# Last four output tiles in emptied weight buffers, the last tile copied by two engines, and a re-planned instruction order

## Chip, cores and metric

The kernel runs on one core of one Trainium2 chip. The metric is the device time of one execution in microseconds; for the kernel before it is 155.75 us (median of 13 runs, 154.97 to 156.91).

The core's engines are PE (TensorE, matrix multiplication, with PEld for its weight loads), DVE (VectorE), ACT (ScalarE), POOL (GpSimd) and SP (SyncE, which issues nearly all transfers here). Each engine works through its own instructions in the order in which they were written for it. Transfers between the chip's main memory (DRAM) and on-chip memory (SBUF) run on 16 DMA queues. PE writes its results to PSUM, which has eight banks.

## What is computed

A gated linear recurrence over 768 steps (4 batches, 8 heads, head size 48), followed by a gated MLP with a mix over the sequence. Cut to what matters:

```python
# q, k, v, alpha: (4, 8, 768, 48)
for t in range(S):
    state = alpha[:, :, t, :, None] * state + np.einsum('bhd,bhe->bhde', k[:, :, t], v[:, :, t])
    y[:, :, t] = np.einsum('bhd,bhde->bhe', q[:, :, t], state)
x = y.transpose(0, 2, 1, 3).reshape(4, 768, 384)

h = np.maximum(x @ w_in, 0.0)                  # w_in: (384, 1024)
u, v = h[..., :512], h[..., 512:]
v_n = (v - mean(v)) / sqrt(var(v) + 1e-6)      # over the last axis
v_s = np.einsum('ts,bsd->btd', w_spatial, v_n) + b_spatial[None, :, None]   # w_spatial: (768, 768)
out = (u * v_s) @ w_out                        # w_out: (512, 384); out: (4, 768, 384), float32
```

## The kernel before

**First stage.** Each batch's sequence is cut into 6 chunks of 128 steps, 24 chunks in all. For each chunk alpha, k, q and v are loaded (`ac`, `kc`, `qc`, `vc`). The decay is handled by logarithms: ACT takes `ln` (`la`), PE sums it along the chunk (`cum`), ACT takes the two exponentials (`binv`, and `cum` in place), POOL multiplies k by one (`kt`), DVE multiplies q by the other (`qt`). PE transposes both (`pt`), the result is copied to SBUF (`kqT`, operation `ev`), PE multiplies them (`sc`), DVE applies the causal mask (`ptm`), and PE forms the chunk's output `y` from the masked scores, v and the state carried over. The carried state is made in three operations of `state_update`: `z` on DVE (line 331, the sum of the old state and the chunk's update), `S` (line 338, the scaling by the chunk's decay, on POOL) and `sb` (line 344, two half copies into `sbd`, on POOL or DVE). Chunks 0 to 5 (batch 0) go in pairs through `pair`, the others singly through `first`. `finish_x` copies `y` out (`xs`), transposes it and stores it as the batch's `xT` (`xe`).

**Second stage.** For each batch PE multiplies `xT` by the two halves of `w_in` (groups `v` and `u`). `v` is normalised (`bn`, `rs`, `vn`), mixed over the sequence by `w_spT` (group `s`), given its bias on DVE (`vsb`) and multiplied by `u` on POOL (`g`, giving `gT`). Group `o` multiplies `gT` by `w_out`; there are 24 output tiles of 128 rows, 6 a batch. All these groups go through the helper `group`, so their matrix multiplications all stand on line 775. Each output tile is copied from PSUM to SBUF by ACT (line 960, recorded as line 207 of the helper `copy`), and SP issues its store (line 967).

**Buffers of output tiles.** `out_tile` (line 935) says where tile n goes. Tiles 0 to 7 go into `raw_w`, a ring of two buffers that held the weights as they were loaded, four tiles to a buffer. Tiles 8 to 10 go into `w_row`, which held `w_spatial`. Tiles 11 to 23 go into `o_sb`, a ring of four buffers, so that a tile from 15 on waits for the store of the tile four before it. The list `free` in `second_o` (line 951) tells the planner of this.

**The order.** Nothing above is issued in the order in which it is written. Every piece of work is an `Op` with the engines that may do it and a planned duration for each (`ENGINES`, line 76, holds some), its dependencies and a priority. `schedule` (line 96) then plans greedily: at each step, of all operations that could start, it takes the one with the smallest planned start (plus half the duration where several engines may do it, plus the operation's own `wait`, which `PATIENCE`, line 75, sets by kind), and emits it on that engine. So a changed number can change the order on every engine. Where PE has a planned gap before `WARM` (40 us), the planner fills it with multiplications of a constant tile `junk` (line 199), whose results are not used.

**Loads in the plan.** `dma` (line 305) makes two operations, the issue on SP and the transfer, with a planned time and a planned latency (`lat`, 1.9 by default). `PIECES` (line 89) says after which load of a chunk each weight is fetched; `w_out` comes after chunk 7's `qc`. The issue of the fetch gets that load's issue as a dependency (`late`, line 1000).

Of the kernel before, what the change touches and what calls it, by code (L numbers as in the profile page):

```python
# [51 lines left out]
class Clock:  # L52
# [19 lines left out]
        return end  # L72


PATIENCE = {"ev": -0.3, "v": -0.1, "g": -0.3, "sb": 0.3, "bb": 0.5, "ln": 0.2, "z": -0.2, "we": -0.1, "S": 0.2, "cast": -0.1, "rs": 0.1, "trk": -0.1, "xs": -0.3}
ENGINES = {
    "kt": {"POOL": 0.87},
    "vb": {"POOL": 0.47, "ACT": 0.42},
    "S": {"POOL": 0.57},
    "sb": {"POOL": 0.79, "DVE": 0.36},  # L80
    "vn": {"DVE": 0.33},
    "xe": {"ACT": 0.38},
# [1 line left out]
    "u": {"ACT": 0.38, "DVE": 0.47},  # L84
    "o": {"ACT": 0.38},
}
PAIRS = (0, 1, 2)
ACT_STATS = ((2, 2), (1, 4), (3, 4))
PIECES = {
    "w_in": ((0, "vc", 0, 0.35), (0, "kc", 2, 0.15)),  # L90
    "w_sp": ((0, "vc", 4, 0.35), (0, "qc", 6, 0.25), (0, "qc", 6, 0.25)),
    "w_out": (0, "qc", 7, 0.25),
}


# [45 lines left out]
def kernel(  # L141
# [14 lines left out]
    B, H, S, D = q.shape  # L156
# [3 lines left out]
    DM = H * D  # L160
    DFF = moe_w_in.shape[1]
    DH = DFF // 2
    NT = S // 128
# [12 lines left out]
    LD, LP, WT, ST = 0.97, 1.46, 2.35, 0.8  # L176
# [28 lines left out]
    def copy(eng, out, in_):  # L205
        if eng == "ACT":
            nc.scalar.copy(out=out, in_=in_)  # L207
        else:
            ENG[eng].tensor_copy(out=out, in_=in_)  # L209
# [81 lines left out]
    def op(key, *args, **kw):  # L291

        users = kw.pop("use", ())
        o = Op(*args, **kw)
        for s in users:
            s.users.append(o)
        ops.append(o)
        made[key] = o
        o.wait = PATIENCE.get(key[0], 0.0)
        return o  # L300

    def got(*keys):
        return [made.get(x) for x in keys]

    def dma(key, us, emit, deps, prio, eng="SP", issue=0.99, lat=1.9):
        o = op(key + ("issue",), eng, issue, emit, deps, prio=prio)
        return op(key, "DMA", us, lambda _: None, [o], prio=prio, lat=lat)
# [9 lines left out]
    def state_update(i, ndeps):  # L317

        c = i % NCH
        st = T[i]  # L320
        P = float(10 * i)
        sbd = sbd_bufs[i % NB]

        def z(_):
            st["state"] = work.tile([128, HP, D], FP32, name="state")
            if c == 0:
                nc.vector.tensor_copy(out=st["state"], in_=st["tp"])
            else:
                nc.vector.tensor_tensor(out=st["state"], in0=st["tp"], in1=T[i - 1]["state"], op=ALU.add)  # L329

        op(("z", i), "DVE", 0.27, z, got(("upd", i), ("S", i - 1), ("sb", i - WK)), prio=P + 8, use=[st["sl_t"]])

        def sf(eng):
            ENG[eng].tensor_tensor(  # L334
                out=st["state"], in0=st["state"], in1=st["bc"][:, :, None].to_broadcast([128, HP, D]),
                op=ALU.mult)

        op(("S", i), ENGINES["S"], None, sf, got(("z", i), ("ebc", i)), prio=P + 8)

        def sb(eng):  # L340
            copy(eng, sbd[0:64, :, 0:D], st["state"][0:64])
            copy(eng, sbd[64:128, :, D:2 * D], st["state"][64:128])

        op(("sb", i), ENGINES["sb"], None, sb, got(("S", i), ("y", i - NB + 1), ("cz", 1)), prio=P + 8.1)

    def finish_x(i):
# [20 lines left out]
        def xe(eng):  # L367
            if c == 0:
                tiles(b)
            to, fr = bt[b]["xT"][:, :, t0:t0 + C], st["xv"]  # L370
            if i // 2 in PAIRS:
                to = to.rearrange("p k (t two) -> p k t two", two=2)
# [6 lines left out]
    def io_users(x, j, back=None):  # L379

        j = j - IO if back is None else j
        if x == "cum":
            return got(("cum", 2 * j), ("cum", 2 * j + 1), ("cump", j, 0), ("cump", j, 1))
        return got((x, 2 * j), (x, 2 * j + 1), (x + "p", j), (x + "p", j, 0), (x + "p", j, 1))
# [205 lines left out]
    def first(i):  # L590
# [3 lines left out]
        st = T[i]  # L594
        P = float(10 * i)

        def load(name, src):
            def emit(_):
                if i % 2 == 0:
                    T[i + 1][name + "2"] = st[name + "2"] = io_pool.tile([128, 2, H, D], FP32, name=name)  # L600
                t = st[name] = st[name + "2"][:, i % 2]
                nc.sync.dma_start(out=t, in_=src[b, :, t0:t0 + C, :].rearrange("h s d -> s h d"))
            return emit

        j = i // 2
        jo = j - NKP
        dma(("ac", i), LD, load("ac", alpha), io_users("ln", j), P)
        dma(("kc", i), LD, load("kc", k), io_users("kt", j), P + 0.1)
        dma(("qc", i), LD, load("qc", q), io_users("qt", j), P + 0.2)
        dma(("vc", i), LD, load("vc", v), io_users("vb", j), P + 0.3)  # L610

        la, kt, qt = [x[j % NKP][:, i % 2].rearrange("p (hp s) d -> p hp s d", s=2) for x in (lap_bufs, ktp_bufs, qtp_bufs)]

# [51 lines left out]
        hold = {}  # L665
# [88 lines left out]
    def group(key, mms, per, deps, prio, evac, eng, dur, edeps=(), parts=2, pdeps=None):  # L754

        hold = {}
        sl = Slot(rings["p2"])
        n = -(-len(mms) // parts)
        prev = None
        for j in range(parts):  # L760
            part = mms[j * n:(j + 1) * n]

            def emit(_, part=part, j=j):
                if j == 0:
                    hold["ps"] = bank(pp_2, [128, 512], FP32, name="ps2")
                for m in part:
                    m(hold["ps"])

            prev = op(key + ("mm", j), "PE", per * len(part), emit,
                      list(deps) + [prev] + (pdeps[j] if pdeps else []),  # L770
                      prio=prio, take=sl if j == 0 else None, use=[sl], cols=per * len(part) * 2350)
        return op(key, eng, dur, lambda e: evac(e, hold["ps"]), [prev] + list(edeps), prio=5.0, use=[sl])

    def mm(out, lhsT, rhs, start, stop):
        return lambda ps: nc.tensor.matmul(out=out(ps), lhsT=lhsT(), rhs=rhs(), start=start, stop=stop)  # L775
# [34 lines left out]
    def second_v(b, tt):  # L810
# [3 lines left out]
        t0 = tt - tt % 2  # L814
        on_act = (b, t0) in ACT_STATS

# [117 lines left out]

    def out_tile(n):

        if n < 8:
            if n % 4 == 0:
                kept["t"] = raws.tile([128, 4 * DM], FP32, name="raw_w")
            return kept["t"][:, n % 4 * DM:(n % 4 + 1) * DM]  # L940
        if n < KEEP:
            return raws.tile([128, S], BF16, name="w_row", bufs=NROW).bitcast(FP32)
        return outp.tile([128, DM], FP32, name="o_sb")

    def second_o(b, tt):
        mms = [mm(
            lambda ps: ps[:, 0:DM], lambda dsl=dsl: bt[b]["gT"][:, dsl, tt * 128:(tt + 1) * 128],
            lambda dsl=dsl: w_out_sb[:, dsl, :], dsl == 0, dsl == NDS - 1) for dsl in range(NDS)]
        hold = {}
        n = b * NT + tt  # L950
        if n < 8:
            free = [made[("cast", "w_out", x)] for x in range(NDS)] + [made[("cast", "w_sp", 2, x)] for x in range(2)]
        elif n < KEEP:
            free = got(("wt", n - 8 + 3))
        else:
            free = got(("st", (n - 4) // NT, (n - 4) % NT)) if n >= KEEP + 4 else []

        def evac(eng, ps):
            hold["o"] = out_tile(n)
            copy(eng, hold["o"], ps[:, 0:DM])  # L960

        Q = 1000.0 + 100 * b + 30 + tt
        group(("o", b, tt), mms, 0.165, [made[("g", b, x, tt // 3)] for x in range(NDS)] + made[("w_out",)], Q, evac,
              ENGINES["o"], None, free, parts=1)

        def store(_):
            nc.sync.dma_start(out=out[b, tt * 128:(tt + 1) * 128, :], in_=hold["o"])

        dma(("st", b, tt), ST, store, got(("o", b, tt)), -1.0, issue=0.8)
        if n < KEEP:  # L970
            late.extend((made[("st", b, tt, "issue")], (x, N - 1, "issue")) for x in ("ac", "kc", "qc", "vc"))
        made[("all", b)] = made[("o", b, tt)]
# [49 lines left out]
    for b in range(B):  # L1022
        for c in range(NCH):
            i = b * NCH + c
            if i // 2 in PAIRS:
                if i % 2 == 0:
                    pair(i // 2)
            else:
                first(i)
            second_v(b, c)  # L1030
            if c == 2 or c == NCH - 1:
                for ft in range(NDS):
                    second_u(b, ft, c // 3)
        if b == 0:
            weights()
            bias()
        for th in range(2):
            for dsl in range(NDS):
                second_s(b, dsl, th)
        for tt in range(NT):  # L1040
            second_o(b, tt)
# [35 lines left out]
```

## Time and profile before

| | |
|---|---|
| Median of 13 runs | 155.75 us (154.97 to 156.91) |
| The profiled execution's own time | 155.77 us |
| Its span, first to last instruction | 154.0 us |
| Mean granted clock of PE | 0.992 |
| Transfers | 28.62 MB, mean 186 GB/s |
| POOL busy | 83.5 us (54%), 141 instructions |
| ACT copies `o_sb<-ps`, 128x384 | 13, mean 477 ns |
| POOL scalings `state<-state,bc`, 128x192 | 20, mean 511 ns |
| DVE sums `state<-tp,state`, 128x192 | 16, mean 350 ns |
| Stores from `o_sb`, issue to landing | 13, median 2.2 us |
| Loads of single chunks, issue to landing | 72, medians 3.9 to 4.1 us |

Times inside the profile count from the first instruction. Busy time of PE is modelled: multiplications are pipelined, so the mean of one (326 ns for a 128x384 one) is longer than the distance from one to the next. "Idle before" and its releaser say what an engine waited for. Other engines than the bounding one may idle at no cost.

### The profile page before, as it was taken

The numbers are of one execution on the slowest core, as the hardware profiler recorded it, in microseconds if no ns is written. First come the engines' busy times: TensorE is split into PE (matmuls) and PEld (weight loads), VectorE is DVE, ScalarE is ACT, GpSimd is POOL, SyncE is SP. The second block draws the span as 40 slices with busy tenths as digits, with TensorE's granted clock in tenths as the row PEclk, the third lists the DMA queues.
The fourth block names the chain that finished last, engine by engine and source line by source line (L and its number), as shares of the span: only waits on it lengthen the run. The fifth ranks groups of instructions, "written<-read, shape, count | busy, mean of one in ns | idle before, by whom it ended". The sixth has DMA issues, their size and how long they took to land.

```text
span 154.0 us, 4579 instructions
## 1 busy us (share of the span) xinstructions
PE 145.0 (94%) x1761; PEld 95.4 (62%) x1761; DVE 123.7 (80%) x268; ACT 110.9 (72%) x273; POOL 83.5 (54%) x141
## 2 busy tenths in 40 slices
PE   7899799999999999999999999999999989999960
PEld 6587567766657566666557575756666646665530
DVE  7666589589999999996888998899979997467900
ACT  3586486899999596899895779899955947860141
POOL 6737337855337888834389497524767851005400
PEclk9999999999999999999999999999999999999996
DMA  4999999999999799989799999999990012400053
GB/s 122 264 314 290 313 237 275 242 273 184 259 210 260 163 217 193 199 166 213 155 193 210 177 201 216 178 201 214 318 345 6 2 51 101 159 0 0 2 195 117
DMA packets 93015, 28.62 MB, mean 186 GB/s; under 512 B 87872, under 2 KB 91456, under 8 KB 92992
## 3 DMA queue, kind: packets, MB, share of 16 engines
q1 hardware_dynamic: 92960, 28.32, 78.5%
q8 instruction: 14, 0.23, 0.6%
q14 instruction: 9, 0.07, 0.2%
q0 software_dynamic: 32, 0.00, 0.0%
HBM read 23.60 MB, written 4.72 MB: 184 GB/s over the span
## 4 chain that ended last, share of the span: by engine, by line
PE 77%; ACT 6%; DVE 5%; DMA 5%; POOL 2%; issue 2%; ACTq 0%; DVEq 0%; POOLq 0%
PE ps L775 42%; PE pt L672 4%; PE pt L702 4%; PE y L363 3%; DMA out_dram<-o_sb 3%; DMA ac<-in_alpha_dram 2%; PE y L730 2%; PE cum L621 2%; PE tp L688 2%; PE y L573 2%; PE ps L199 2%; POOL gT L928 2%; PE y L724 2%; PE ps L430 2%; PE ps L495 2%
## 5 line engine op out<-in xcount | busy, mean ns | idle before, releaser
L775 PE MATMUL ps<-w_spT,vn 128*128 128x384 bf16 x192 | 36.1, 326 | 0.0
L928 POOL TENSOR_TENSOR gT<-vsb,uT 128x384 bf16<-128x384 f32 x28 | 25.8, 928 | 17.4 <-DVE vsb L915 17.0
L713 DVE TENSOR_TENSOR ptm<-pt,mask 128x512 bf16<-128x512 f32 x36 | 23.4, 681 | 1.7 <-PE pt L702 1.6
L775 PEld LDWEIGHTS <-vn 128*128 128x128 bf16 x192 | 17.1, 97 | 10.2 <-issue 0.2
L645 POOL TENSOR_TENSOR kt<-kc,binv 128x384 bf16<-128x384 f32 x18 | 16.5, 916 | 11.4 <-ACT bc L640 6.2
L334 POOL TENSOR_TENSOR state<-state,bc 128x192 f32<-128x192 f32 x20 | 10.2, 511 | 21.5 <-DVE state L329 13.5
L775 PE MATMUL ps<-w_in,xT 128*128 128x512 bf16 x72 | 18.9, 380 | 0.1
L207 ACT CAST x_sb<-y 128x384 bf16<-128x384 f32 x24 | 11.4, 479 | 10.1 <-PE y L730 7.2
L775 PE MATMUL ps<-w_out_sb,gT 128*128 128x384 bf16 x96 | 18.6, 326 | 0.0
L775 PE MATMUL ps<-xT,w_in 128*128 128x384 bf16 x96 | 18.4, 326 | 0.0
L915 DVE TENSOR_TENSOR vsb<-ps,bsp_bc 128x384 f32<-128x384 f32 x31 | 16.3, 548 | 2.1 <-PE ps L775 1.2
L207 ACT COPY o_sb<-ps 128x384 f32<-128x384 f32 x13 | 6.2, 477 | 11.3 <-PE ps L775 9.7
L837 DVE BATCH_NORM_STATS2 stats<-v_sb 128x6 f32<-128x512 bf16 x18 | 12.3, 684 | 1.5 <-ACT v_sb L213 1.4
L213 ACT ACTIVATE v_sb<-ps 128x512 bf16<-128x512 f32 x18 | 10.7, 596 | 3.9 <-PE ps L775 3.4
L207 ACT COPY xT<-y 128x384 bf16<-128x384 bf16 x24 | 11.4, 486 | 1.4 <-PE y L363 1.1
L209 POOL CAST sbd<-state 64x192 bf16<-64x192 f32 x30 | 11.0, 367 | 1.3
L199 PEld LDWEIGHTS <-junk 128*128 128x128 bf16 x112 | 10.4, 108 | 2.0 <-DVE junk L240 1.1
L775 PEld LDWEIGHTS <-gT 128*128 128x128 bf16 x96 | 8.4, 97 | 5.0
L775 PEld LDWEIGHTS <-w_in 128*128 128x128 bf16 x96 | 8.4, 97 | 4.9
L867 DVE TENSOR_SCALAR vn<-v_sb,mvs,rstd 128x512 bf16<-128x512 bf16 x24 | 10.7, 483 | 0.8 <-ACT rstd L860 0.7
L215 DVE TENSOR_SCALAR uT<-ps 128x384 bf16<-128x384 f32 x16 | 8.5, 552 | 3.4 <-PE ps L775 3.3
L775 PEld LDWEIGHTS <-xT 128*128 128x128 bf16 x72 | 6.1, 97 | 6.8 <-ACT xT L207 2.4
(128 smaller groups left out, 314.2 us busy)
## 6 DMA issues: line engine op xcount, KB each, us to landing
ac<-in_alpha_dram SPq DMA_DIRECT2D x18, 192.0 KB, 4.0
kc<-in_k_dram SPq DMA_DIRECT2D x18, 192.0 KB, 4.1
qc<-in_q_dram SPq DMA_DIRECT2D x18, 192.0 KB, 4.1
vc<-in_v_dram SPq DMA_DIRECT2D x18, 192.0 KB, 3.9
out_dram<-o_sb SPq DMA_DIRECT2D x13, 192.0 KB, 2.2
raw_w<-in_moe_w_spatial_dram SPq DMA_DIRECT2D x3, 768.0 KB, 5.7
raw_w<-in_moe_w_in_dram SPq DMA_DIRECT2D x2, 768.0 KB, 8.0
out_dram<-raw_w SPq DMA_DIRECT2D x8, 192.0 KB, 2.8
```

What stands on the lines that cost most here:

```text
L199: nc.tensor.matmul(out=flat[:, 0:cols], lhsT=junk[:, 0:128], rhs=junk[:, 0:cols], start=True, stop=True)
L207: nc.scalar.copy(out=out, in_=in_)
L209: ENG[eng].tensor_copy(out=out, in_=in_)
L213: nc.scalar.activation(out=out, in_=in_, func=AF.Relu)
L334: ENG[eng].tensor_tensor(out=st["state"], in0=st["state"], in1=st["bc"][:, :, None].to_broadcast([128, HP, D]), op=ALU.mult)
L645: ENG[eng].tensor_mul(out=kt[:, :, :, 0:D], in0=quad(st["kc"]), in1=st["binv"])
L713: nc.vector.tensor_tensor(out=st["ptm"][:, s], in0=st[f"pt{s}"], in1=mask4, op=ALU.mult)
L775: return lambda ps: nc.tensor.matmul(out=out(ps), lhsT=lhsT(), rhs=rhs(), start=start, stop=stop)
L837: nc.vector.bn_stats(out=stats, in_=d["v_sb"][:, tt, :])
L867: nc.vector.tensor_scalar(out=d["vn"][:, t, :], in0=d["v_sb"][:, t, :], scalar1=d["mvs"][:, t, 0:1], scalar2=d["rstd"][:, t:t + 1], op0=AL ...
L915: nc.vector.tensor_tensor(out=hold["vs"], in0=ps[:, 0:TH], in1=bsp_bc[:, th, :], op=ALU.add)
L928: ENG[eng].tensor_tensor(out=bt[b]["gT"][:, dsl, cols], in0=hold["vs"], in1=bt[b]["uT"][:, dsl, cols], op=ALU.mult)
```

## The change

```diff
-PATIENCE = {"ev": -0.3, "v": -0.1, "g": -0.3, "sb": 0.3, "bb": 0.5, "ln": 0.2, "z": -0.2, "we": -0.1, "S": 0.2, "cast": -0.1, "rs": 0.1, "trk": -0.1, "xs": -0.3}
+PATIENCE = {"ev": -0.3, "kt": -0.1, "v": -0.1, "sb": 0.3, "bb": 0.5, "ln": 0.2, "z": -0.2, "we": -0.1, "S": 0.2, "cast": -0.1, "rs": 0.1, "trk": -0.1, "xs": -0.3, "xe": -0.2}
 ENGINES = {
...
-    "S": {"POOL": 0.57},
+    "S": {"POOL": 0.57, "DVE": 0.27},
...
+NUDGE = {
+    ("o", 3, 0, "mm", 0): -0.15,
+    ("bn", 0, 1): -0.6,
+    ("upd", 2): -0.15,
+    ("qtp", 2, 0): 0.3,
+    ("v", 0, 3): -0.3,
+    ("kt", 6): 1,
+    ("S", 2): -0.3,
+    ("vbp", 0, 0): -1,
+    ("g", 1, 1, 1): -1,
+    ("u", 1, 3, 0): 1,
+    ("cast", "w_in", 0, 0): 0.3,
+    ("rs", 0, 0): -0.6,
+    ("qc", 0): 1,
...
+    ("y", 0): -1,
+    ("g", 3, 0, 0): -0.6,
+}
+LATE = 2.9
 PIECES = {
...
-    "w_out": (0, "qc", 7, 0.25),
+    "w_out": (0, "kc", 7, 0.15),
 }
...
-        o.wait = PATIENCE.get(key[0], 0.0)
+        o.wait = PATIENCE.get(key[0], 0.0) + NUDGE.get(key, 0.0)
...
-        dma(("ac", i), LD, load("ac", alpha), io_users("ln", j), P)
+        dma(("ac", i), LD, load("ac", alpha), io_users("ln", j), P, lat=LATE)
...
     def out_tile(n):
 
-        if n < 8:
+        if n < 8 or n >= B * NT - 4:
             if n % 4 == 0:
                 kept["t"] = raws.tile([128, 4 * DM], FP32, name="raw_w")
             return kept["t"][:, n % 4 * DM:(n % 4 + 1) * DM]
...
         elif n < KEEP:
             free = got(("wt", n - 8 + 3))
+        elif n >= B * NT - 4:
+            free = got(*[("st", 0, x) for x in range(4)])
...
         def evac(eng, ps):
             hold["o"] = out_tile(n)
-            copy(eng, hold["o"], ps[:, 0:DM])
+            if n < B * NT - 1:
+                copy(eng, hold["o"], ps[:, 0:DM])
+                return
+            half = DM // 2
+            copy("ACT", hold["o"][:, 0:half], ps[:, 0:half])
+            copy("DVE", hold["o"][:, half:DM], ps[:, half:DM])
```

Tiles 20 to 23 share one `raw_w` buffer, the third use of that ring for output, after tiles 0 to 3. Tile 23 is copied in two halves of 192 columns, one by ACT and one by DVE; the planner counts it as one ACT operation of 0.38 as before. The state scaling `S` may go to DVE. `NUDGE` adds to the `wait` of 30 single operations, 20-odd of them of batch 0. `LATE` replaces the planned latency of 1.9 by 2.9 for the four loads of each chunk from 6 on (`ac` is shown; `kc`, `qc` and `vc` are alike). `w_out` may be fetched from chunk 7's `kc` on.

More of the change, by code (lines that the diff above doesn't have):

```diff
@@ L86 @@
 }
+NUDGE = {
[12 more added lines that the diff above has]
+    ("qc", 0): 1,
+    ("sb", 20): -0.6,
+    ("g", 0, 2, 1): -0.6,
+    ("g", 3, 0, 1): 0.6,
+    ("vbp", 1, 1): 0.6,
+    ("sc", 0, 0): -0.6,
+    ("v", 0, 4): -1.5,
+    ("s", 3, 3, 1): 0.3,
+    ("xs", 1): -0.15,
+    ("S", 14): 0.3,
+    ("ktp", 0, 0): -1.5,
+    ("S", 22): 0.6,
+    ("st", 1, 4): 0.6,
+    ("st", 0, 5): 0.3,
+    ("ev", "k", 1, 0): -1,
+    ("cast", "w_in", 1, 2): -0.3,
+    ("y", 0): -1,
+    ("g", 3, 0, 0): -0.6,
+}
 PAIRS = (0, 1, 2)
+LATE = 2.9
 ACT_STATS = ((2, 2), (1, 4), (3, 4))
@@ L606, in first @@
         jo = j - NKP
-        dma(("ac", i), LD, load("ac", alpha), io_users("ln", j), P)
-        dma(("kc", i), LD, load("kc", k), io_users("kt", j), P + 0.1)
-        dma(("qc", i), LD, load("qc", q), io_users("qt", j), P + 0.2)
-        dma(("vc", i), LD, load("vc", v), io_users("vb", j), P + 0.3)
+        dma(("ac", i), LD, load("ac", alpha), io_users("ln", j), P, lat=LATE)
+        dma(("kc", i), LD, load("kc", k), io_users("kt", j), P + 0.1, lat=LATE)
+        dma(("qc", i), LD, load("qc", q), io_users("qt", j), P + 0.2, lat=LATE)
+        dma(("vc", i), LD, load("vc", v), io_users("vb", j), P + 0.3, lat=LATE)
         la, kt, qt = [x[j % NKP][:, i % 2].rearrange("p (hp s) d -> p hp s d", s=2) for x in (lap_bufs, ktp_bufs, qtp_bufs)]
```

## The prediction

> **What bounds the kernel now.** I read four views in this order: the page, the busy time by stretches of 5 us, the chain of work that ended last, and the waits. The page first.
>
> ```profile
> span 154.0 us, 4579 instructions
> PE 145.0 (94%) x1761; PEld 95.4 (62%) x1761; DVE 123.7 (80%) x268; ACT 110.9 (72%) x273; POOL 83.5 (54%) x141
> PE   7899799999999999999999999999999989999960
> DVE  7666589589999999996888998899979997467900
> PEclk9999999999999999999999999999999999999996
> ```
>
> PE is the bound nearly everywhere, at full clock. The exceptions are the head (slices 1 to 10) and the last two slices. The stretches say how much a better order could win. The columns are PE, PEld, DVE, ACT and POOL busy, clock, DMA share, GB/s.
>
> ```profile
> 40.00:45.00 5.00, 4.96 (x56) 3.06 (x55) 4.59 (x11) 4.75 (x13) 0.91 (x1) 1.00 1.02 275
> ...
> 75.00:80.00 5.00, 4.88 (x49) 2.71 (x49) 4.46 (x12) 4.54 (x13) 3.12 (x7) 1.00 0.81 162
> ...
> 120.00:125.00 5.00, 4.33 (x55) 2.60 (x54) 4.89 (x12) 3.73 (x8) 3.89 (x6) 1.00 0.01 3
> ```
>
> Every other stretch from 40 to 145 us reads 5.00 for PE, so idle there is 0.04 + 0.12 + 0.67 = 0.83 us in 105. Nothing larger can be won by order in that part. In the head PE is partly busy with fill: multiplications of a constant that the planner puts into PE's planned gaps. The same view for their line alone (PE and PEld):
>
> ```profile
> 5.00:10.00 5.00, 2.31 (x24) 1.82 (x24) 1.00 1.27 266
> 10.00:15.00 5.00, 2.50 (x29) 2.08 (x27) 1.00 1.18 314
> 15.00:20.00 5.00, 0.32 (x5) 0.12 (x2) 1.00 1.14 302
> 20.00:25.00 5.00, 2.54 (x25) 1.91 (x25) 1.00 1.04 247
> 25.00:30.00 5.00, 1.22 (x11) 0.95 (x11) 1.00 0.99 266
> ```
>
> That is 94 fills. The chain has 18 of them in 1.56 us, 0.087 us each, so about 8 us of PE's time in the head is not work; the DMA share stays near 1 there, so loads limit how much of it can be filled. Now the end of the chain and two of the waits.
>
> ```profile
> 132.78 12.45 PE ps L775 x74
> 145.23 0.02 issue
> 145.25 0.49 ACT o_sb L207
> 145.74 0.02 issue
> 145.76 3.88 DMA out_dram<-o_sb
> 149.64 0.02 issue
> 149.66 0.04 ACTq L207
> 149.70 0.04 issue
> 149.74 0.95 ACT o_sb L207 x2
> ```
> ```profile
> ACT o_sb L207 <- DMA out_dram<-o_sb: 1.6, 1, 1.6
> SPq L1072 <- DMA out_dram<-o_sb: 1.4, 1, 1.4
> ```
>
> PE's last multiplication ends at 148.95 (the timeline has six from 147.81 for 1.14 us). ACT nevertheless copies the last two tiles only at 149.74, because tile 22 takes the buffer of tile 18, whose store was issued at 145.76 and landed 3.88 us later. This is what sets the end: copy, store, landing, 1.1 us of closing.
>
> **The last four tiles in the weight space.** Tiles 20 to 23 leave the ring of four `o_sb` buffers for a `raw_w` buffer whose previous use is the stores of tiles 0 to 3. The stores of tiles 0 to 7 were issued from 106.94 over 4.82 us, so nothing is waited for near 148 us. ACT copies stand at 146.39, 147.04 and 147.69, one per 0.65 us (four multiplications). So tile 22's copy starts at 148.34 instead of 149.74 and ends at 148.82, and tile 23 is ready for copying at 148.99 instead of being copied from 150.22.
>
> The stores come next on SP. The fourth of the six ends its issue at 149.13 (147.54 plus 1.59 for two). The fifth and sixth were issued from 150.24 over 1.11 us, the sixth from 150.71. Now they follow the fourth directly. Their issue price is what decides: 0.33 us at best, 1.12 us at worst (both on the store line), and 0.60 us in the eight stores of tiles 0 to 7, issued back to back (4.82 / 8). Back to back is the nearest row, so I take 0.60: the sixth starts at 149.75, a gain of 0.96 us. At 0.33 it starts at 149.48; without the long third issue at 149.36, a gain of 1.35. At 1.12 it starts at 150.25 and takes 0.48 longer than its 0.64 now, a gain of about 0.
>
> There is a second limit. The completion records of tile 18's store show 15 of 16 parts landed by 147.61 and the last at 149.64; the last parts of the next three landed at 150.11, 150.59 and 151.05, so one queue runs late and works off a store per 0.47 us. Two more behind it land at 151.99, where the last landing now is at 152.86: 0.87 us at most while that lag stays. I take **-0.9 us**, between 0 and -1.35.
>
> **The last tile by two engines.** It was one ACT copy of 0.48 us. Half on ACT lies between 0.176 (the 128x4 activation) and 0.477 (128x384), so 0.33; half on DVE is the row `state<-tp 128x192 f32`, 0.346. Side by side they end at 149.34, one after the other at 149.67. No row shows two engines reading one bank at once. I take side by side, since neither depends on the other. Either end is before SP is free at 149.75, so the edit is worth **0**; if SP issues in 0.33, the serial case costs 0.2.
>
> The kernel before has each output bank emptied by one engine. The Trainium skill, "PSUM — Partial Sum Buffer", section "PSUM bank collisions raise a hardware error", says that ScalarE and VectorE reading one bank in the same partitions at once collide, disjoint columns included, and that software has to keep them apart. That speaks against this edit: kept apart, the last copy would end at 149.67 rather than 149.34, still under the store queue.
>
> **Landings and the weight load.** `LATE` makes the plan assume loads of single chunks (6 to 23) 1 us later (0.97 + 2.9 = 3.87 us; the page has 3.9 to 4.1). No `la` activation of these chunks waits for anything (its group has 0.0 idle), so the covers are loads that come early: the fourth `la` runs at 49.23 on a load issued at 40.32. Worth 0; without that cover each load would cost up to 1 us. The `w_out` load may now be issued after chunk 7's `kc`, not its `qc`. Those were issued at 30.47 and 31.10, and `w_out` at 45.47, so this bound does not bind: 0. If it did move ahead on SP, the loads behind it would start 0.54 us (its issue) to 3 us later (768 KB at about 250 GB/s in that part of the page's transfer row); the 9 us between issue and use cover that too, and the casts of `w_out` on POOL and ACT from 53.9 on would come earlier.
>
> **The state scaling may go to DVE, and 30 operations are nudged.** POOL does 20 scalings at 0.51 us. On DVE the nearest row is the state sum over the same 128x192, 0.35. Gain: the chain state sum, scaling, `sbd`, `y`. PE's 0.67 us of idle in 120 to 125 ends with `sbd`; taking 0.16 and a hand-over off that chain is worth about 0.2. Cost: DVE load, priced below as a rival. The nudges remove no instruction; 20-odd concern the first batch. By the rows the whole re-plan lies between -8 us (every fill gone) and the rival's +2. I take **-0.2**, since PE has only 0.83 us to give after 40 us and the head is held by loads.
>
> **Sum.** -0.9 + 0 + 0 - 0.2 = -1.1 us. The profiled span goes from 154.0 to 152.9; the run lasted 155.77 (1.77 around the span), which is the median (155.75) within 0.02. Forecast: 154.65, written 154.6; its own range is 154.1 to 155.3.
>
> **Rivals.**
> - *The head packs better.* Half of the 36 fills between 20 and 30 us go: 18 x 0.087 = 1.6 us more. For: most nudges are there, and PE streams without a break afterwards, so a gain lasts to the end. Against: DMA share 1.0 to 1.3. Time 153.1.
> - *DVE becomes the bound.* Summed over the 18 stretches from 35 to 125 us DVE is busy 82.4 of 90 (92%). Its densest 25 us, 40 to 65, read 4.59 + 4.78 + 4.70 + 5.00 + 4.82 = 23.9 (95.6%). Some 16 scalings of 0.35 add 5.6 us: 88.0 / 0.956 = 92.0, 2.0 us longer, from the point where DVE's added work passes 3.6 us (0.956 x 90 - 82.4). What speaks against it: `sbd` halves (ten on DVE at 0.364 us, 3.6 us in all) can go back to a freer POOL. With the end's -0.9 it is 156.85: slower.
> - *The gain is eaten.* Stores issue at 1.12 us, or a new stall of about 0.9 us arises, for example a copy on an in-order engine queued behind one that is late. Time 155.6, no change. For: PE's order was already almost free of gaps, so a new order is more likely to open some than to close more.
>
> **How the numbers follow.** Forecast 0.38, head 0.25, eaten 0.15, DVE 0.22. A change under 0.3% (0.47 us) can't be told from none. Forecast and head lie below 155.28 but for a sliver, hence faster 0.62, same 0.15, slower 0.23. The range is 152.8 to 156.9: it reaches 0.3 us past the head case and just past the DVE case, and leaves out about 0.08 below (nearly all fills of 20 to 30 us gone) and 0.10 above.
>
> **What would show it.** Right: no ACT wait for a store at the end; the sixth store issued about 1 us after PE's last multiplication, not 1.8. Right for the re-plan: PE's last end near 148.8, fills still near 94 after 5 us. Wrong: PE ending after 150 with DVE near 5.00 in every stretch (DVE rival), PE ending near 147 with fewer fills (head), or the sixth store's issue still behind 150.2.

## The result, and the profile after

The change made the kernel slower: 157.50 us (median of 11 runs) against 155.74 (48 runs). The ratio is 1.0131, with an interval of 1.0111 to 1.0152. The profiled span went from 154.0 to 155.8 us.

From the page of the kernel after:

```profile
span 155.8 us, 4579 instructions
PE 146.0 (94%) x1766; PEld 96.1 (62%) x1766; DVE 128.1 (82%) x273; ACT 108.1 (69%) x269; POOL 82.8 (53%) x141
PE   7999799999999999897989998999999999999990
```

Before, PE's row had no digit under 9 from slice 6 to slice 32. Now slices 17, 19, 21 and 25 read 8, 7, 8 and 8 (3.9 us each, so from 62 us on). The stretches of 5 us place the gaps (PE, PEld, DVE, ACT, POOL busy, clock, DMA share, GB/s):

```profile
65.00:70.00 5.00, 4.30 (x59) 2.84 (x58) 4.18 (x10) 3.04 (x8) 1.01 (x2) 1.00 1.00 194
70.00:75.00 5.00, 4.19 (x55) 2.68 (x53) 3.69 (x9) 4.79 (x15) 1.72 (x3) 1.00 1.04 206
75.00:80.00 5.00, 4.16 (x48) 2.49 (x46) 4.85 (x11) 3.74 (x13) 3.00 (x7) 1.00 0.93 184
...
95.00:100.00 5.00, 4.31 (x46) 2.59 (x43) 4.58 (x8) 3.98 (x11) 3.49 (x5) 1.00 1.11 221
```

These four stretches lack 3.04 us of PE; before they lacked 0.12. The wait list of PE names one releaser for each gap (total, times, longest):

```profile
PE ps L808 <- ACT uT L246: 0.9, 2, 0.7
PE ps L808 <- ACT xT L240: 0.8, 1, 0.8
PE pt L705 <- DVE qt L688: 0.7, 1, 0.7
PE pt L735 <- DVE kqT L242: 0.7, 1, 0.7
```

Four different operations on two engines are late. So no one engine became the bound; PE's instructions stand in an order in which, at four places, it needs a result that is not there yet. The end of the chain:

```profile
135.93 16.14 PE ps L808 x97
152.07 0.02 issue
152.10 0.33 ACT raw_w L240
152.43 0.02 issue
152.45 0.36 DVE raw_w L242
```

The store between the copies is gone from it. PE stops at 152.06 (before: 148.95), 3.1 us later, and from there to the end 3.7 us pass instead of 5.1. So +3.1 - 1.3 = +1.8 us of span. Of the 3.1 us, 2.3 are PE's added idle between 40 and 145 us (3.12 against 0.83). Five more fills (117 against 112) at 0.087 make 0.4 (an estimate from the chain's 0.087 us each). The remaining 0.4 I can't place in this view, whose multiplications are modelled.

The two copies of the last tile stand one after the other: 0.33 + 0.02 + 0.36 us for what one copy did in 0.48. DVE had been free for 2.3 us and waited for ACT. In the trace its copy waits for the semaphore that ACT's copies raise, so the built program puts the two halves in a row, though no line of the kernel asks for it:

```profile
DVE raw_w L242 <- ACT raw_w L240: 2.3, 1, 2.3
```

### The profile page after: what moved, and what is told of

Its sections match the earlier page's. It is cut to its first block, busy times and chain, and to the rows that moved or that the text cites. A ratio compares the mean times of both kernels' runs of the same rounds, so it can differ in the third digit from the quotient of the medians.

```text
span 155.8 us, 4579 instructions
## 1 busy us (share of the span) xinstructions
PE 146.0 (94%) x1766; PEld 96.1 (62%) x1766; DVE 128.1 (82%) x273; ACT 108.1 (69%) x269; POOL 82.8 (53%) x141
## 4 chain that ended last, share of the span: by engine, by line
PE 67%; DVE 7%; ACT 6%; issue 2%; POOL 1%; DVEq 0%
PE ps L808 45%; PE pt L705 5%; PE pt L735 3%; PE y L396 3%; PE y L763 2%; PE tp L721 2%; PE cum L654 2%; PE y L757 1%; PE y L606 1%; DVE vn L900 1%; DVE vsb L948 1%; PE ps L818 1%; ACT v_sb L855 1%; DVE ptm L746 1%; ACT sq L866 1%
## 5 line engine op out<-in xcount | busy, mean ns | idle before, releaser
L808 PE MATMUL ps<-w_spT,vn 128*128 128x384 bf16 x192 | 36.7, 326 | 0.7 <-ACT uT L246 0.7
L961 POOL TENSOR_TENSOR gT<-vsb,uT 128x384 bf16<-128x384 f32 x27 | 24.6, 920 | 19.2 <-DVE vsb L948 18.8
L367 POOL TENSOR_TENSOR state<-state,bc 128x192 f32<-128x192 f32 x17 | 8.7, 510 | 19.4 <-DVE state L362 8.7
L232 PEld LDWEIGHTS <-junk 128*128 128x128 bf16 x117 | 10.9, 108 | 2.2 <-DVE junk L273 1.1
L900 DVE TENSOR_SCALAR vn<-v_sb,mvs,rstd 128x512 bf16<-128x512 bf16 x24 | 11.9, 525 | 0.1
L242 DVE COPY kqT<-pt 128x1024 bf16<-128x1024 bf16 x16 | 10.8, 681 | 1.2 <-PE pt L705 1.1
L242 POOL CAST sbd<-state 64x192 bf16<-64x192 f32 x30 | 10.4, 346 | 2.0 <-DVE state L367 0.8
L240 ACT COPY o_sb<-ps 128x384 f32<-128x384 f32 x9 | 4.4, 483 | 10.0 <-PE ps L808 9.8
```

Source lines behind the costliest of these rows:

```text
L232: nc.tensor.matmul(out=flat[:, 0:cols], lhsT=junk[:, 0:128], rhs=junk[:, 0:cols], start=True, stop=True)
L367: ENG[eng].tensor_tensor(out=st["state"], in0=st["state"], in1=st["bc"][:, :, None].to_broadcast([128, HP, D]), op=ALU.mult)
L900: nc.vector.tensor_scalar(out=d["vn"][:, t, :], in0=d["v_sb"][:, t, :], scalar1=d["mvs"][:, t, 0:1], scalar2=d["rstd"][:, t:t + 1], op0=AL ...
L961: ENG[eng].tensor_tensor(out=bt[b]["gT"][:, dsl, cols], in0=hold["vs"], in1=bt[b]["uT"][:, dsl, cols], op=ALU.mult)
```

## The experiments

Ratios are against the kernel before on the same chip, with 95% intervals. The runs come from several chips (medians of before 155.27 to 155.58 us in these experiments), so rows are compared by their ratios. To separate the order from the other edits, some runs have the planner's result written out: a list of every operation with its engine and the fills in front of it, which replaces the planning. With the list of before, the instructions of before come out on every engine; with that of after, those of after.

```diff
-    schedule(ops, fill, 2.0, WARM)
+    for key, eng, cols in ORDER:
+        fill.extend(cols)
+        left.pop(key).emit(eng)
```

| Run | Order | Tail | Median us | Ratio | Interval |
|---|---|---|---|---|---|
| e1 | before, written out | new buffers, one copy | 154.86 | 0.9969 | 0.9942 to 0.9996 |
| e2 | before, written out | new buffers, two copies | 154.62 | 0.9944 | 0.9920 to 0.9967 |
| e3 | after, written out | old | 157.56 | 1.0137 | 1.0100 to 1.0173 |
| t1 | after, written out | new buffers, one copy | 157.28 | 1.0115 | 1.0100 to 1.0130 |
| after | after | new buffers, two copies | 157.50 | 1.0131 | 1.0111 to 1.0152 |

**The new buffers, in the old order (e1).**

```diff
-        if n < 8:
+        if n < 8 or n >= B * NT - 4:
```

> The order of before, written out instruction by instruction, with only the new buffers for tiles 20 to 23 (one copy each, all on ACT). If the loss is the new order's (theory): PE ends near 149.0 as before, no ACT wait for a store, sixth store issued near 149.6 instead of 150.7; about 1.1 to 1.4 us under before, 154.3 to 154.6. If the new buffers are what costs (rival): 155.7 or more.

The gain is there, but about 0.5 us instead of 1.1 to 1.4. Timeline of this run:

```profile
147.04 2.84 SPq L2092 DMA_DIRECT2D out_dram<-raw_w  x4
147.19 0.48 ACT L1329 COPY raw_w<-ps 128x384 f32<-128x384 f32 x1 [0.17 <-PE ps L1898]
147.84 0.48 ACT L1329 COPY raw_w<-ps 128x384 f32<-128x384 f32 x1 [0.17 <-PE ps L1898]
148.49 0.48 ACT L1329 COPY raw_w<-ps 128x384 f32<-128x384 f32 x1 [0.17 <-PE ps L1898]
```

ACT no longer waits for a store: its copies follow PE at 0.65 us each and the last ends at 148.97. SP is now last. It needs 2.84 us for four stores, 1.37 of them for the first, so the sixth store is issued only at 149.47, 1.02 us after PE's last multiplication (148.45). The second limit that the prediction named is there as well: in this trace's completion records the last of the 16 parts of the six stores land at 149.35, 149.82, 150.30, 150.77, 151.24 and 151.71, one per 0.47 us, while the other 15 parts of the sixth store had landed by 151.53. So the late queue, not SP alone, sets the end here.

**Both tail edits, in the old order (e2).**

```diff
+            half = DM // 2
+            copy("ACT", hold["o"][:, 0:half], ps[:, 0:half])
+            copy("DVE", hold["o"][:, half:DM], ps[:, half:DM])
```

> The run before plus the last tile copied in two halves. In the trace of after the DVE half starts only when the ACT half has ended (0.33 + 0.02 + 0.36 us instead of one copy of 0.48). If that order comes from the bank and not from chance: 0.1 to 0.25 us slower than the run with one copy, 154.4 to 154.8. If the halves can run side by side with this order: 0.1 faster than that run.

The halves ran one after the other here too (0.33, then 0.36 from 149.08), but the run is not slower than e1; the intervals overlap. SP hides them: the fifth store's issue ends at 149.54 and the halves at 149.44. My expectation had overlooked that cover. In this trace no part of the last four stores is late by more than 0.04 us, so the lag of e1 comes and goes from run to run.

**The old tail, in the new order (e3).**

> The order of after, written out, with the old buffers and one copy of the last tile. If the new order alone is the loss: PE ends near 152.1 as in after, the ACT wait for a store comes back, 158.0 to 159.0, about 1 us over after. Rival (the new tail makes part of the loss): 157.5 or less.

It takes as long as after. Its chain shows why the new buffers win next to nothing there:

```profile
147.20 4.18 DMA out_dram<-o_sb
...
151.48 0.43 ACT o_sb L1329
151.91 0.04 issue
151.95 0.48 ACT o_sb L1329
```

The new order issues tile 18's store 4.5 us before PE's end (147.20, PE ends at 151.74); in before it was 3.2 us. The landing still releases the copy of tile 22, but only 0.3 us late: the copies start at 151.48 and 151.95, where t1, without the wait, has 151.19 and 151.84. The new order alone accounts for the loss, and for most of the shorter tail (from PE's end to the end of the span 3.8 us here, 3.7 in after, 5.1 in before).

**One copy, in the new order (t1).**

> After, its order written out, with tile 23 copied in one piece by ACT. In after the sixth store is issued at 152.84, 0.55 us after SP was free, when the DVE half ends. If the two halves in a row are what it waits for: the store 0.23 us earlier and the time 157.1 to 157.4. Rival (halves cost nothing): 157.5 as after.

157.28 against 157.50; the intervals overlap, so the difference is not settled by these two runs alone. The trace agrees with it: ACT copies the last tile from 151.84 for 0.48 us and the sixth store is issued at 152.35, 0.53 us after PE's end. In after that distance is 0.78 us, because SP is free and waits for the DVE half.

**The scalings back on POOL, in the new order (e4).** In the written list of after, the scalings of chunks 1, 9 and 15 change from DVE to POOL; for chunk 9:

```diff
-    (('S', 9), 'DVE', ()),
+    (('S', 9), 'POOL', ()),
```

> After, its order written out, with the three state scalings that went to DVE (chunks 1, 9 and 15) put back on POOL at the same places of the order. If DVE's 0.64 us scalings make the stalls at 65 and 77 us: PE idle after 40 us falls by 1 us or more and the time to 156.5 or less. If the stalls come from the order as a whole: within 0.3 us of after, 157.2 to 157.8, or slower, since POOL takes 0.51 us each at a place that was planned for 0.27.

156.56 us (1.0077, 1.0044 to 1.0110): 0.9 us of the loss goes away. PE's last multiplication ends at 150.51 instead of 152.06. The gap at 65 us has closed and the one at 95 us has shrunk:

```profile
65.00:70.00 5.00, 4.95 (x74) 3.44 (x74) 4.16 (x9) 3.86 (x10) 0.50 (x1) 1.00 0.87 169
70.00:75.00 5.00, 4.10 (x47) 2.33 (x44) 3.84 (x9) 4.81 (x16) 2.32 (x4) 1.00 1.10 220
75.00:80.00 5.00, 4.26 (x59) 2.74 (x55) 4.59 (x11) 3.72 (x12) 2.76 (x7) 1.00 0.98 189
95.00:100.00 5.00, 4.74 (x58) 3.02 (x59) 4.19 (x8) 3.98 (x12) 3.02 (x5) 1.00 0.96 191
```

PE's whole idle after 40 us, which the expectation names, can't be compared here: 15 of PE's records are missing from this trace (1751 against 1766). The gaps at 70 and 75 us remain, and PE still waits for `xT` (0.8 us) and `uT` (0.7); they are the order's. What had opened the first is seen in after's timeline of DVE, and then of POOL:

```profile
62.20 0.64 DVE L367 TENSOR_TENSOR state<-state,bc 128x192 f32<-128x192 f32 x1
62.77 1.29 DVE L242 CAST sbd<-state 64x192 bf16<-64x192 f32 x2
64.09 0.69 DVE L746 TENSOR_TENSOR ptm<-pt,mask 128x512 bf16<-128x512 f32 x1
...
90.56 1.02 DVE L367 TENSOR_TENSOR state<-state,bc 128x192 f32<-128x192 f32 x1
```
```profile
62.72 0.91 POOL L678 TENSOR_TENSOR kt<-kc,binv 128x384 bf16<-128x384 f32 x1
...
90.46 0.91 POOL L678 TENSOR_TENSOR kt<-kc,binv 128x384 bf16<-128x384 f32 x1 [0.21 <-ACT binv L666]
```

Planned were 0.27 us for the scaling and 0.36 for the two `sbd` halves. They took 0.64 and 1.29, with POOL working on SBUF at the same time. PE then waited for `qt`, which stands behind them on DVE (0.7 us in the list above). In e4 the `sbd` halves are nearly as slow without the scaling before them:

```profile
61.45 0.36 DVE L1485 TENSOR_TENSOR state<-tp,state 128x192 f32<-128x192 f32 x1 [0.18 <-PE tp L1844]
61.73 1.13 DVE L1364 CAST sbd<-state 64x192 bf16<-64x192 f32 x2
...
64.36 0.54 DVE L1811 TENSOR_TENSOR qt<-qc,cum 128x384 bf16<-128x384 f32 x1
```

From the state sum to `qt` it is 2.91 us there and 3.75 in after (61.81 to 65.56): the scaling's place on DVE is worth 0.84 us of delay, of which about 0.3 is its being stretched (0.64 against the 0.35 that it takes in m1 below). The scaling of chunk 15 took 1.02 us beside another `kt`.

**The scalings on DVE, in the old order (m1).** The same three entries in the list of e2, the other way round.

```diff
-    (('S', 9), 'POOL', ()),
+    (('S', 9), 'DVE', ()),
```

> The counterpart of the run with the scalings back on POOL: the order of before with both tail edits, and the scalings of chunks 1, 9 and 15 on DVE at their old places. If a scaling on DVE costs by itself, wherever it stands (0.64 us in after, beside POOL's work): about 0.9 us over the old order with both tail edits, 155.3 to 155.8. If it hurts only in the new order: within 0.3 of that run, 154.4 to 154.9.

154.78 us (0.9963, 0.9936 to 0.9991), as e2. A scaling on DVE does not cost by itself. In this run the three took the least that any did, and no POOL operation ran beside any of them:

```profile
L1457 DVE TENSOR_TENSOR state<-state,bc x3: 347/348/348, 15.0 to 93.6; 128x192 f32<-128x192 f32 x3
```

**The parts of the re-plan, one at a time.** These runs plan anew, with both tail edits (r6 with one copy) and with the new entry of `w_out` in `PIECES`. "Places" counts the 298 PE operations that stand elsewhere than in the old order. "Planned end" is the planner's own reckoning of PE's last operation, not a measurement. The old order has 0 and 142.9.

| Run | What of the re-plan is in | Places | Planned end | Median us | Ratio | Interval |
|---|---|---|---|---|---|---|
| r1 | scaling may go to DVE | 13 | 142.9 | 154.09 | 0.9910 | 0.9873 to 0.9947 |
| r6 | the same, one copy | 13 | 142.9 | 153.79 | 0.9894 | 0.9872 to 0.9915 |
| x4 | patience of `g` alone | 149 | 143.8 | 155.68 | 1.0016 | 0.9999 to 1.0034 |
| x2 | latency 2.4 | 215 | 144.1 | 156.00 | 1.0048 | 1.0013 to 1.0083 |
| r2 | latency 2.9 | 217 | 144.1 | 156.35 | 1.0051 | 1.0017 to 1.0085 |
| r3 | new patience | 145 | 145.0 | 156.54 | 1.0072 | 1.0043 to 1.0100 |
| r5 | latency 2.9, patience | 212 | 143.7 | 157.18 | 1.0107 | 1.0090 to 1.0125 |
| after | all, with the nudges | 193 | 144.1 | 157.50 | 1.0131 | 1.0111 to 1.0152 |
| x1 | latency 0.9 | 182 | 143.4 | 157.73 | 1.0148 | 1.0116 to 1.0180 |
| r4 | all but the nudges | 212 | 143.7 | 158.47 | 1.0192 | 1.0125 to 1.0259 |
| x3 | patience turned round | 214 | 147.7 | 159.80 | 1.0291 | 1.0253 to 1.0329 |

They start from after with the old `PATIENCE`, the old `ENGINES` entry of `S`, `LATE = 1.9` and an empty `NUDGE`, which plans the old order of PE (0 of 298 places differ). From there r1 has

```diff
-    "S": {"POOL": 0.57},
+    "S": {"POOL": 0.57, "DVE": 0.27},
```

and r2

```diff
-LATE = 1.9
+LATE = 2.9
```

r3 has the new `PATIENCE` line in full:

```diff
-PATIENCE = {"ev": -0.3, "v": -0.1, "g": -0.3, "sb": 0.3,
+PATIENCE = {"ev": -0.3, "kt": -0.1, "v": -0.1, "sb": 0.3,
...
-"xs": -0.3}
+"xs": -0.3, "xe": -0.2}
```

r5 joins r2 and r3, and r4 all three.

> After with the old patience, the old planned latency and no nudges: what is left of the re-plan is that the scaling may go to DVE (the plan puts four there). Theory that DVE is what costs: 155.3 or more. Rival (the plan puts them where DVE has room): 154.4 to 154.9, as the old order with both tail edits.

> After with the old patience, scalings on POOL alone and no nudges: what is left is the planned latency of 2.9. In the traces no activation of these loads waits for one, so a plan that holds work back for them can only lose. If that is what opens PE's idle of 65 to 80 us: 155.5 to 157. If the latency does nothing: 154.4 to 154.9.

> After with the old planned latency, scalings on POOL alone and no nudges: what is left is the new patience by kinds of operation. If the latency alone is what costs: within 0.3 us of the old order with both tail edits, 154.4 to 154.9. If the new patience costs too: 155.3 or more.

> After without the 30 nudges. If the nudges are what costs: 155 or less. If they win back a part of what the latency, the patience and the DVE scaling cost: 158 or more. If they do nothing: 157.2 to 157.8.

> After without the nudges and with scalings on POOL alone: the new latency and the new patience together. After without the nudges is at 158.5, the latency alone at 156.35. If the DVE scaling makes the difference of 2 us: about 156.4. If the patience makes it: about 158.4.

The DVE option alone costs nothing and by the medians gains 0.5 us; r1's interval still overlaps that of e2. It closes the gap that the prediction had pointed at, between 120 and 125 us. e2 first, then r1:

```profile
120.00:125.00 5.00, 4.28 (x58) 2.70 (x57) 4.88 (x12) 3.74 (x8) 3.64 (x6) 1.00 0.06 20
```
```profile
120.00:125.00 5.00, 5.00 (x65) 3.16 (x64) 4.93 (x12) 3.75 (x8) 4.16 (x8) 1.00 0.06 22
```

The latency alone costs about 1.7 us against e2 (1.0051 - 0.9944, of 155.5), the patience alone 2.0, both together 2.5. With them in, the DVE option costs 1.3 more (r4 against r5), where alone it cost nothing (the two intervals just touch). The nudges lead back from 158.47 to 157.50; those two intervals overlap, so their effect is likely but not shown. The `w_out` entry is in r1, which is not slower than e2, so it costs nothing that shows.

A loss from latency and from patience alike left two readings: that these numbers are wrong, or that any other order which this planner makes is slower than the old one. Moving them the other way tells the two apart: x1 and x2 by the latency, x3 and x4 by the patience.

```diff
-LATE = 1.9
+LATE = 0.9
```
```diff
-LATE = 1.9
+LATE = 2.4
```
```diff
-PATIENCE = {"ev": -0.3, "v": -0.1, "g": -0.3, "sb": 0.3,
+PATIENCE = {"ev": -0.3, "kt": 0.1, "xe": 0.2, "v": -0.1, "g": -0.6, "sb": 0.3,
```
```diff
-PATIENCE = {"ev": -0.3, "v": -0.1, "g": -0.3, "sb": 0.3,
+PATIENCE = {"ev": -0.3, "v": -0.1, "sb": 0.3,
```

> Both tail edits, old patience, scalings on POOL, no nudges, and the planned latency moved the other way, from 1.9 to 0.9. If a longer planned latency costs because it holds the loads' users back (theory A): this one does not hold them back, 154.2 to 154.9, as the old order. If any other order costs because the old numbers were tuned to the chip (theory B): 155.3 or more.

> The same with a planned latency of 2.4, half way to the change's 2.9, which alone gave 156.35. Theory A (held-back users cost in proportion): 155.2 to 155.8. Theory B (any other order costs its own amount): no place between the two ends need come out, 155.3 to 157.

> Both tail edits, old latency, scalings on POOL, no nudges, and the three changes of patience turned round (kt +0.1, xe +0.2, g -0.6). The changed patience alone gave 156.54. If those three steps go the wrong way (theory A): 154.9 or less. If any other order costs (theory B): 155.3 or more, as the changed patience did.

> Both tail edits, old latency, scalings on POOL, no nudges, and of the three changes of patience only that g loses its -0.3. If g is what the changed patience costs: 156 to 157. If it lies in kt and xe: 154.2 to 154.9. Theory B has 155.3 or more for it, since 653 places of the written order change.

The second reading holds for the nine orders made here. A latency lowered by 1.0 loses more than one raised by 1.0. Half the step gives nearly the order of the whole step (215 and 217 places), and the same time. The patience turned round is the slowest of all. Every run that moved over 140 of the 298 PE operations (nine orders) is slower than e2, by 0.7 to 3.5%; the two that moved 13 are not.

That the old order was fitted to the chip is one way to read this; the column of planned ends gives another, which the runs don't rule out. By the planner's own reckoning, too, PE ends later in all nine (143.4 to 147.7 against 142.9), so a part of each loss is in the plan: 1.2 us of it in after. The plan doesn't give the rest, nor the ranking: x1, planned to end at 143.4, is slower than r2, planned to end at 144.1.

What PE waits for differs. In x1:

```profile
PE pt L704 <- DVE ptm L715: 1.3, 1, 1.3
...
PE y L726 <- DVE sbd L211: 1.0, 1, 1.0
```

In x3 it waits for ACT's `xT` (1.3 us) and DVE's `uT` (1.1). In r2 and x2 PE's wait list is nearly that of e2 (0.7 us for `sbd`, 0.3 for `ptm`), and there are six more fills (118 against 112, about 0.5 us at 0.087 each); where the rest of their loss goes is not seen in these views. Which operation makes each of these plans worse was not followed up.

**The fastest (r6).** r1 with one copy of the last tile.

```diff
-            if n < B * NT - 1:
+            if n < B * NT:
```

> The fastest so far (scalings allowed on DVE, old patience and latency, no nudges, new buffers) with one copy of tile 23. In that run's trace the sixth store is issued at 148.70, 0.35 us after the fifth one's issue has ended. If the halves in a row delay it: 0.2 us less, 153.7 to 154.0. Rival: 154.1.

153.79 us, 1.1% under the kernel before (0.9894, 0.9872 to 0.9915) and 2.4% under after. The intervals of r1 and r6 overlap, so a gain by the one copy is not shown. The sixth store follows the fifth at once here (issues at 148.15 and 148.65), where in r1 it waited for the DVE half; but in this trace SP's third issue took 1.25 us, and the sixth store stands 0.91 us after PE's end, against 0.77 in r1.

## Why the prediction was wrong

Forecast were 154.6 us and a gain; the kernel lost 1.8 us.

- **The failed step is the re-plan, "I take -0.2".** By e3 it measures +2.1 us (1.0137) with the old tail, and by after against e2 2.9 us with the new one. PE's last multiplication was to end near 148.8 and ended at 152.06; its idle after 40 us rose from 0.83 to 3.12 us instead of shrinking. I read the 0.83 us as a cap on what an order can win and did not read it as the sign of an order against which another would lose, as all nine re-plans here that moved over 140 PE operations do. That sentence stood only in the rival "the gain is eaten", at about 0.9 us and 0.15 of the chance. Which move in the order costs what stays open, but for the three scalings (0.9 us, e4).
- **"Landings ... worth 0" was wrong in kind.** No `la` of these chunks waits for a load, as I said (0.0 us idle in before and in after; after's wait list does put two waits of POOL's `kt` down to loads, 1.5 and 0.4 us, but none of PE's). But a planned latency is not a wait: the planner moved 217 of 298 PE operations because of it, and that costs 1.7 us alone. The cover that I named (loads that come early) covers nothing of this. The change of `PATIENCE` I did not price at all; it costs 2.0 us alone.
- **The DVE rival had the right sign with the wrong cause.** DVE's load rose from 123.7 to 128.1 us, but only three scalings went there, not sixteen, and DVE is not full in the gaps (4.18, 3.69 and 4.85 of 5). PE ended after 150, as this rival's sign had it, but DVE was not near 5.00 in every stretch. The three cost 0.9 us in this order by their place in DVE's queue and by the time two of them took beside POOL (0.64 and 1.02 us), not by the sum of load; the same three at their old places, with POOL idle beside them, cost nothing (m1). Where the option is the only change, by the medians it helps, and through the chain that I had named: the idle before `sbd` at 120 to 125 us went to 0 (r1). I had taken 0.35 for one from a row that reads PSUM; the runs have 0.35 where POOL is idle, and 0.36 to 1.02 beside it.
- **The new buffers: right mechanism, size 0.5 to 0.9 instead of 0.9** (e1, e2). SP's issues count, as argued: in e1 1.37 us for the first of four, then 0.38 to 0.40, in place of 0.60 each. So does the late queue, with the 0.47 us per store that I had read (e1). In the new order the buffers are worth 0.1 to 0.3 us, within the intervals (e3 against after and t1), since that order itself moves tile 18's store forward.
- **The two copies: I took side by side, and they ran in a row.** The cost is about 0 where SP is busy (e2), as the sum had it, and where SP is free the sixth store stands 0.24 us further behind PE's end (after against t1), the 0.2 of the serial case; by the times this is not settled. The Trainium skill's rule ("PSUM — Partial Sum Buffer", section "PSUM bank collisions raise a hardware error": two engines on one bank are to be kept apart) speaks of just this case. In all 13 traces with the two copies the second reader starts only when the first has ended, 0.35 us after the first's start, and after's trace shows the semaphore that makes it wait. What would happen without that wait no run here shows. The rule was the better guide than the lack of a dependency in the kernel's text.
- **The upper bound of the re-plan, +2, was right in size (+2.1), by luck:** it was worked out from sixteen scalings that fill DVE, and three went there, which cost 0.9. And the range added the tail's full -0.9 to it, as if the two were independent (156.9). With the tail's gain void in the new order the same bound gives 157.8.
- **Two readings were off, without weight.** The 94 fills count one twice where it lies in two stretches: 88 of before's 112 start after 5 us, and 93 of after's 117. Of the 30 nudges 19 concern the first batch, not 20-odd. The head did not pack better.

## What to carry to other kernels

When nearly all time of the bounding engine is used, its order is already a good one, and a re-plan is a new draw: price it by the losses of other draws (here 0.7 to 3.5%, against 0.8 us of idle to win), not by the best case. Look at the planner's own end first: it had PE 1.2 us later in the new order. A number in a planner can move operations on every engine, so it is not free just because no wait shows it. Test edits of buffers and of engines with the order held fixed, and only then let the planner move.

## What the hardware showed

- DVE operations on SBUF can be stretched while POOL works. In after the three scalings took 347, 637 and 1023 ns, the first with POOL idle and the others beside its `gT` and `kt`; the 128x2 scaling of the sums, 156 and 160 ns with POOL idle, took 0.88 us from 75.84 and ended with POOL's `kt` (75.78 to 76.69). It is not so each time: in r1 a scaling took 358 ns with POOL at work beside it. The masks, which read PSUM, took 655 to 692 ns with POOL busy or idle.
- An operation's time on DVE thus depends on where the plan puts it, which is one way in which a plan made with fixed durations misses.
- SP's issue of a 192 KB store took 0.33 us (after) to 1.62 us (r3) in the same place, the third of the last six. Nothing in these runs tells why.
